# Threshold attention followed by a squared-ReLU layer on one Trainium2 core: scores a step ahead in five banks, queries loaded by sweep, values grouped by block

## The chip, the cores and the metric

The kernel runs on one core of a Trainium2 chip. A core has five engines that run their own instruction streams and meet only through semaphores: TensorE (PE in the profile, with its weight loads shown as PEld), VectorE (DVE), ScalarE (ACT), GpSimd (POOL) and SyncE (SP), whose queue here does little but issue DMAs. TensorE writes its products to PSUM, a memory of 128 partitions and 8 banks of 512 float32 each; SBUF holds everything else on the chip.

The metric is device time in microseconds (us) of one execution, as the median of several runs. A profile is one execution taken by the hardware profiler; its span runs from the first to the last recorded instruction.

## What is computed

Attention over 8 batches and 8 heads, 576 tokens, head dimension 64, in float32, whose weights are cut off below the row maximum less tau, and then a layer on the joined heads:

```python
scores = scale * np.matmul(q, k.transpose(0, 1, 3, 2))
thresh = np.max(scores, axis=-1, keepdims=True) - tau
scores = np.where(scores >= thresh, scores, -1000000000.0)
scores = scores - np.max(scores, axis=-1, keepdims=True)
attn = np.exp(scores)
attn = attn / (np.sum(attn, axis=-1, keepdims=True) + 1e-09)
attn_out = np.matmul(attn, v)
...
x = np.ascontiguousarray(attn_out.transpose(0, 2, 1, 3)).reshape(B * S, H * D)
h = x @ w_in
r = np.maximum(h, 0.0)
g = r * r
return g @ w_out
```

w_in is 512 x 2048, w_out 2048 x 512. There are 4608 tokens.

## The kernel before

**Visits and steps.** Heads are handled in pairs, two heads of 64 dimensions filling the 128 partitions. The 576 queries of a pair are five blocks: four of 128 (i = 0 to 3) and one of 64 (i = 4, where both heads share the partitions). A visit `n` is a pair with a list of blocks, and a step `s` is one block of one visit. The first batch is swept twice: visits 0 to 3 take blocks 0 and 1 (steps 0 to 7), visits 4 to 7 take blocks 2, 3 and 4 (steps 8 to 19). So the first 256 tokens of x are complete for all heads early, and the layer's work on them (chunk 0) can begin. Visits 8 to 10 take all five blocks (steps 20 to 34). In visits 0 to 10 the attention weights are turned by TensorE; from visit 11 on they are turned by DVE and DMAs ("by DMA"), and from visit 12 two visits are paired (`late_step`). The change touches visits 0 to 10.

**What a step does.** In order of the data: `scores` (L258; matmuls of L273, or L266 for block 4) puts 128 x 576 scores of each of the two heads u into PSUM; `maxima` (L310, DVE) takes the row maxima; `exponents` (ACT) makes the bias and the threshold (L322, L323) and the exponents of each head (L325); `threshold` (L337 to L340, DVE) sets the weights under the threshold to zero, by reading the scores in PSUM again, and sums them; `divide` (L345, L347, POOL) divides. Two steps later `turn` (L378) turns the weights: nine 128 x 128 transposes of TensorE in three parts of three (L386), each part copied from its PSUM bank to `wT` by ACT (L387). A step after that `mix` (L499) multiplies values with turned weights (L502) and `put` copies the sums to `xT` (L485). `prep(n)` transposes the queries and keys of a visit on DVE (L247), after `load_qk(n)` has loaded them (L179, L182); `load_v` (L230) loads values; `split_left` (L242) lays out the queries of block 4.

**Order.** It is written out by hand: an engine executes its instructions in the order in which the program issues them, and the framework puts in the semaphore waits that the data and the reuse of buffers need. The loop at L1096 writes one step after the other. In it a step issues its own scores, then the first two parts of the turn of two steps before with their copies, then its exponents, values, the third part, and threshold and division.

**PSUM.** `big` is all eight banks. Before step 10 (`early()`, L865) the scores of a step lie in banks 0 to 3 (two banks for each head, `pairs`); step 1 uses 4 to 7. Turns and values take banks 4 and 5 in alternation (`take("tx", ...)`), the second part of a turn 6 or 7. The table `AT` (L113) has four areas of 576 columns, one after the other from column 128: they span banks 0 to 4 and cross their borders. Before, only the late steps use it.

**Rounding.** The layer's weights arrive in 32 pieces, and each is brought to float32 on the way (`round_weights`, L138): stage 0 is two ACT instructions (L149, L150), stages 1 and 2 one of DVE each (L152, L154), stage 3 and the end one of POOL each (L156, L158). `end_rounding` then asks for the piece three further on. The list `pieces` says how many a step rounds: in steps 2, 4 and 6 one, from step 8 on one or two.

**The layer's work** is cut in pieces that `fill` puts between the steps' instructions at the pace of `rate` (L885). Chunk j becomes available in the step in which the last value group it needs is made (`chunk_at`); the first is step 10. `min(chunk_at)` is that step.

The lines of the timetable of value groups, in which x is a block and 3 the lag in steps:

```python
mixed = {x: (x, 3) for x in range(NBLK + 1)}
...
mixes[s + lag] = (n, cols)
```

Of the kernel before, what the change touches and what calls it, by code (L numbers as in the profile page):

```python
# [19 lines left out]
def kernel(  # L20
# [140 lines left out]
    def rows_of(n):  # L161
        return rows_in[n % 2 if n <= 2 * HP else 0]
# [3 lines left out]
    def rows_32(t, n, m):  # L166

        b, h = divmod(visits[n][0], HP)
        return t[b, 2 * h + m // 2, :, (m % 2) * 32:(m % 2) * 32 + 32].rearrange("(c p) d -> p c d", p=32)

    def load_qk(n):


        for x, t in ((rows_of(n)[1], k), (rows_of(n)[0], q)):
            for m in range(4):
                src, to = rows_32(t, n, m), x[m * 32:(m + 1) * 32, :, :]
                queue = nc.scalar if n == 0 and m % 2 else nc.sync
                last = REST // 32 if t is k and m >= 2 and not by_dma(n) else 0
                queue.dma_start(out=to[:, last:, :], in_=src[:, 0:S // 32 - last, :])  # L179
                if last:  # L180
                    queue = nc.gpsimd if n == 0 else nc.sync
                    queue.dma_start(out=to[:, 0:last, :], in_=src[:, S // 32 - last:, :])  # L182
# [61 lines left out]
    def prep_part(t, n):  # L244
        to, rows = (qT, rows_of(n)[0]) if t is q else (kT[n % 2], rows_of(n)[1])
        arrived(rows)
        nc.vector.transpose(to, rows.rearrange("p c d -> p (c d)"))  # L247

    def prep_left():
        arrived(q_left)  # L250
# [7 lines left out]
    def scores(s):  # L258


        vis, i = steps[s]
        n = 2 if i < NBLK else 1
        sc = [(second if s == 1 else pairs)[u] for u in range(n)]
        if i == NBLK:
            for half in range(2):
                nc.tensor.matmul(sc[0][:, half, 0:HALF], qmid, kT[vis % 2][:, half * HALF:(half + 1) * HALF], start=True, stop=True)  # L266
        else:
            halves = [(half, u) for half in range(2) for u in range(n)]
            if early():
                halves.sort(key=lambda x: x[1])  # L270
            for half, u in halves:
                rows = slice(u * D, (u + 1) * D)
                nc.tensor.matmul(sc[u][:, half, 0:HALF], qT[rows, i * P:(i + 1) * P],  # L273
                                 kT[vis % 2][rows, half * HALF:(half + 1) * HALF], start=True, stop=True)
        maxima(s, [x[:, :, 0:HALF] for x in sc])
# [96 lines left out]
    def keep_bank(what):  # L372
# [2 lines left out]
        kept[what] = used["bank"]  # L375
        return to

    def turn(vis, i, part):  # L378

        w = weights[vis, i][0]  # L380
        ps = take("mm", (6, 7)) if early() and part == 1 else take("tx", (4, 5))
        ps = ps.rearrange("p (c n) -> p c n", n=P)
        if i < NBLK:
            for n in range(3):
                c = 3 * part + n
                nc.tensor.transpose(ps[:, n, :], w.rearrange("p u k -> p (u k)")[:, c * P:(c + 1) * P], ident)  # L386
            nc.scalar.copy(wT[:, 2 * i:2 * i + 2, 3 * part:3 * part + 3, :].rearrange("p g c q -> p c g q"),  # L387
                           ps[:, 0:3, :].rearrange("p c (g q) -> p c g q", g=2))
        elif part < 2:
            rows = slice(part * D, (part + 1) * D)  # L390
            for c in range(NBLK):
                at = part * REST + c * P
                nc.tensor.transpose(ps[:, c, 0:D], w[rows, 0, at:at + P], ident[rows, rows])
            at = part * (NBLK + 1)
            nc.scalar.copy(wT[:, 2 * NBLK, at:at + NBLK, :], ps[:, :, 0:D])
        else:

            for rows, keys in ((slice(0, D), slice(S - REST, S)), (slice(D, P), slice(0, REST))):
                nc.tensor.matmul(ps[rows, 0, 0:D], w[rows, 0, keys], ident[rows, rows], start=True, stop=True)
            nc.scalar.copy(wT[:, 2 * NBLK, NBLK, :], ps[:, 0, 0:D])  # L400

    blocks = {}
    outside = {}
# [95 lines left out]
    def mix(n, cols):  # L499

        def term(ps, u, c, at, rows=slice(0, P), first=False, last=False):
            nc.tensor.matmul(ps[u * D:(u + 1) * D, :], vs[n % 2][rows, u * (NBLK + 1) + c, :],  # L502
                             wT[rows, at // REST:(at + ps.shape[1]) // REST, NBLK if c == NBLK else u * (NBLK + 1) + c, :],
                             start=first, stop=last)

        above, below = slice(0, D), slice(D, P)
        arrived(vs[n % 2])
        if not by_dma(n):
            ps = take("tx", (4, 5))[:, 0:cols.stop - cols.start]
            for c in range(NBLK + 1):  # L510
                for u in range(2):
                    term(ps, u, c, cols.start, first=(c == 0), last=(c == NBLK))
            put(n, cols.start, ps, False)
            return
        n1, n2 = 2 * P + REST, 2 * P
        at = ODD if paired(n) and n % 2 else ONE
        one, two = bank[0], bank[4]
        groups = (one[:, 0:n1], at, (above, below)), (two[:, 0:n2], TWO, (below, above))
        for ps, x, _ in groups:
            for c in range(NBLK):  # L520
                for u in range(2):
                    term(ps, u, c, x, first=(c == 0))

        for ps, x, places in groups:
            for u, rows in enumerate(places):
                term(ps, u, NBLK, x, rows, last=True)
        put(n, 0, one[:, ONE - at:ONE - at + 2 * P], True)
        left = ODD if at == ODD else LEFT - at
        put(n, NBLK * P, one[:, left:left + REST], False)
        put(n, 2 * P, two[:, 0:n2], True)  # L530
# [295 lines left out]
    def by_dma(n):  # L826

        return n >= 3 * HP - 1
# [7 lines left out]
    for s, (n, i) in enumerate(steps):  # L836

        if by_dma(n):
            mixed = {visits[n][1][-1]: (0, 3 if n % 2 else 4)}
        else:  # L840
            mixed = {x: (x, 3) for x in range(NBLK + 1)}
        if i in mixed:
            first, lag = mixed[i]
            cols = slice(first * P, S if by_dma(n) else min((i + 1) * P, S))
            mixes[s + lag] = (n, cols)
            g_ = visits[n][0]
            if g_ % HP == HP - 1:
                complete[s + lag] = g_ // HP * S + cols.stop
# [6 lines left out]
            j += 1  # L855
    PIECE_US = 1.76
    VALUES_US = 4.8
    SCORES_US = 1.25
    RESERVE = 3 * PIECE_US
    waiting = deque()  # L860
# [24 lines left out]
    def rate(s):  # L885


        if s < out_from:
            return PIECE_US * sum(x[2] == 0 for x in waiting) / (out_from - s)
        have = PIECE_US * len(waiting) - state["left"]  # L890
        best = 1e9
        at = s
        for e in sorted(chunk_at) + [END]:
            if e > s:
                have += sum(other(x) for x in range(at, e))
                at = e
                best = min(best, (have - (RESERVE if e < END else 0)) / (e - s))
                have += PIECE_US * sum(len(pieces_of(x)) for x in chunk_at.get(e, ()))
        return max(best, 0.0) - other(s)

    def other(s):

# [32 lines left out]
    pieces, left = [], n_pieces  # L935
    for s, (n, i) in enumerate(steps):
        if s < HP * FIRST:
            x = int(n > 0 and i == 0)
        else:
            x = 2 if (n, i) in ((2 * HP - 2, FIRST + 1), (2 * HP - 1, FIRST + 1), (2 * HP, FIRST)) else 1  # L940
        pieces.append(min(x, left))
        left -= pieces[-1]
# [59 lines left out]
    for i in range(RAW):  # L1002
        load_weights(i)
    prep(0)
    nc.vector.tensor_scalar(out=ntau8, in0=ntau8, scalar1=-1.0 / SCALE, scalar2=None, op0=ALU.mult)
    keep_busy(20)
    done = 0
    rounded_by = [0]
# [15 lines left out]
    def late_step(s):  # L1024
# [67 lines left out]
        if valued:  # L1092
            at_least(2, made)
            state["left"] = max(state["left"], -PIECE_US / 2)

    for s in range(END + 1):  # L1096
        state["step"] = s
        if s >= first_late:
            assert 4 not in kept.values()
            late_step(s)  # L1100
            continue
# [4 lines left out]
        if on:  # L1106
# [10 lines left out]
                load_qk(n + 1)  # L1117
            if now:
                round_weights(now[0], 0)
            if s != 1:  # L1120
                scores(s)
                after()
                some_later("gpsimd")
        old = steps[s - 2] if 2 <= s < NST + 2 and not by_dma(steps[s - 2][0]) else None
        at_once = now or old or early()
        lay = on and last and more and not by_dma(n) and s != 1
        if old:
            turn(*old, 0)
            turn(*old, 1)
        if on:  # L1130
            exponents(n, i)
            if s and by_dma(steps[s - 1][0]):
# [18 lines left out]
            for j in chunk_at.get(s, ()):  # L1151
                add_chunk(j)
        if old:
            turn(*old, 2)
        state["free"] = s > first_dma
        if s == 0:
            scores(1)
            prep(1)
        smooth = s > first_dma + 2 and s not in mixes
        some_later("vector")  # L1160
        some_later("gpsimd")
# [77 lines left out]
```

## Time and profile before

| what | value |
|---|---|
| runs | 1335.18, 1333.57, 1335.2 us (median 1335.18) |
| the profiled execution's own time | 1333.83 us |
| its span | 1332.0 us |
| mean granted TensorE clock | 0.994 |
| start of the scores of steps 2, 3, 4, 5 | 14.70, 21.55, 28.81, 33.60 us |
| of steps 6, 7, 8, 9 | 38.80, 43.99, 49.19, 54.39 us |
| of steps 10 and 11 | 59.73, 64.23 us |

The last three rows are the starts of the matmuls of L273 and L266 in the timeline. In the page "busy" is the time in which an engine executes; a busy TensorE is not one at its peak. A digit of the forty slices is the busy share of a fortieth of the span in tenths, and in the row of the clock the share of full speed that was granted. The chain follows the work back from the last instruction, at each step to what released it. In the timeline the columns are start, duration, engine, line, operation, output and input, count, and in brackets the idle time of the engine before it with what ended it.

### The profile page before, as it was taken

What the parts mean: (1) busy time and instruction counts of PE and PEld (TensorE: products, weight loads), DVE (VectorE), ACT (ScalarE), POOL (GpSimd) and SP (SyncE); (2) the same over time, 40 slices, a digit from 0 to 9 for tenths busy, and PEclk for the clock granted to TensorE, in tenths of its full rate; (3) what the DMA queues carried; (4) which work ended last, traced back from release to release, by engine and by line L of the source; (5) the groups of instructions that cost most, each with busy time, mean ns of one, the idle gap of its engine ahead of it and who ended that gap; (6) DMA issues with size and microseconds to landing.
All of it is one profiled execution on the core that took longest, in us unless ns stands there. A gap on an engine that the chain in (4) does not pass through costs nothing.

```text
span 1332.0 us, 25215 instructions
## 1 busy us (share of the span) xinstructions
PE 1295.4 (97%) x9112; PEld 1078.0 (81%) x9112; DVE 927.9 (70%) x2026; ACT 583.0 (44%) x1357; POOL 786.0 (59%) x915
## 2 busy tenths in 40 slices
PE   7898899999999999999999999999999999999998
PEld 5676556888787979797878878888897988889997
DVE  6877776877777878787777776868687877632131
ACT  4776674235262625343534343434443443421321
POOL 4689875775755565474665665747474747454351
PEclk7999999999999999999999999999999999999999
DMA  8764531648786968776766776676686767520000
GB/s 159 160 153 117 144 91 36 159 111 184 166 196 140 214 152 199 167 172 161 167 155 157 163 179 166 168 149 172 148 186 143 178 150 161 161 70 6 12 17 16
DMA packets 330126, 186.69 MB, mean 140 GB/s; under 512 B 291441, under 2 KB 291473, under 8 KB 323601
## 3 DMA queue, kind: packets, MB, share of 16 engines
q1 hardware_dynamic: 317696, 116.87, 46.5%
q0 software_dynamic: 10000, 67.92, 12.8%
q8 instruction: 72, 1.18, 0.4%
q10 hardware_dynamic: 2304, 0.29, 0.2%
q14 instruction: 54, 0.43, 0.1%
HBM read 109.22 MB, written 68.42 MB: 133 GB/s over the span
## 4 chain that ended last, share of the span: by engine, by line
PE 86%; DVE 4%; ACT 3%; POOL 2%; DMA 2%; issue 1%; SPq 0%; ACTq 0%; DVEq 0%; POOLq 0%
PE big L659 29%; PE big L765 28%; PE big L502 10%; PE big L289 8%; PE big L548 3%; PE big L273 3%; PE big L730 2%; PE big L386 2%; DVE st L310 1%; ACT wT L387 1%; DMA wT<-aside 1%; DVE w L337 1%; ACT w L325 1%; DMA aside<-turned 1%; POOL w L347 1%
## 5 line engine op out<-in xcount | busy, mean ns | idle before, releaser
L337 DVE SCALAR_TENSOR_TENSOR w<-big,st,w 128x576 f32<-128x576 f32 x269 | 207.1, 805 | 96.8 <-ACT w L325 96.5
L310 DVE TENSOR_REDUCE st<-big 128x1 f32<-128x576 f32 x288 | 204.2, 748 | 93.8 <-PE big L289 61.7
L347 POOL TENSOR_SCALAR w<-w,st 128x576 f32<-128x576 f32 x269 | 246.6, 926 | 26.4 <-DVE st L340 21.4
L765 PE MATMUL big<-wo,gsum 128*128 128x256 f32 x1088 | 243.8, 382 | 0.0
L765 PEld LDWEIGHTS big<-wo,gsum 128*128 128x128 f32 x1088 | 204.4, 190 | 37.0 <-issue 8.1
L659 PE MATMUL big<-xT,w_in_sb 128*128 128x128 f32 x1536 | 187.4, 277 | 1.3 <-DVE g L671 1.2
L659 PEld LDWEIGHTS big<-xT,w_in_sb 128*128 128x128 f32 x1536 | 178.5, 192 | 10.6 <-issue 8.1
L765 PE MATMUL big<-wo,g 128*128 128x256 f32 x816 | 185.3, 382 | 0.1
L325 ACT ACTIVATE w<-big,st 128x576 f32<-128x576 f32 x269 | 183.8, 734 | 0.0
L765 PEld LDWEIGHTS big<-wo,g 128*128 128x128 f32 x816 | 151.6, 190 | 26.1 <-issue 6.5
L502 PE MATMUL big<-wT,vs 128*64 128x128 f32 (+5 forms) x1700 | 164.2, 355 | 8.3 <-ACT wT L387 4.2
L502 PEld LDWEIGHTS big<-wT,vs 128*64 128x64 f32 (+1 forms) x1700 | 97.1, 137 | 72.0 <-issue 20.7
L322 ACT ACTIVATE st<-st 128x2 f32<-128x2 f32 (+1 forms) x148 | 30.3, 205 | 258.2 <-DVE st L310 257.1
L345 POOL TENSOR_SCALAR st<-st 128x2 f32<-128x2 f32 (+1 forms) x148 | 35.2, 238 | 169.3 <-DVE w L337 163.5
L408 POOL DMA_DIRECT2D aside<-turned x50 | 29.9, 597 | 177.9 <-DVE turned L437 173.7
L671 DVE TENSOR_TENSOR g<-big,g 128x512 f32<-128x512 f32 x96 | 64.7, 676 | 82.4 <-PE big L659 76.8
L289 PE MATMUL big<-kT,qT 64*128 64x256 f32 (+3 forms) x768 | 106.9, 416 | 0.0
L289 PEld LDWEIGHTS big<-kT,qT 64*128 64x128 f32 x768 | 84.5, 186 | 14.5 <-issue 5.0
L667 ACT ACTIVATE g<-g 128x512 f32<-128x512 f32 x96 | 60.2, 628 | 62.9 <-DVE g L671 62.7
L538 POOL TENSOR_TENSOR gsum<-g 128x512 f32<-128x512 f32 x34 | 46.2, 1358 | 69.8 <-ACT g L668 69.6
L668 ACT ACTIVATE g<-g 128x512 f32<-128x512 f32 x128 | 80.7, 630 | 4.1
L431 DVE STREAM_TRANSPOSE turned<-w 128x512 f32<-128x512 f32 x100 | 70.2, 702 | 0.0
(114 smaller groups left out, 2039.0 us busy)
## 6 DMA issues: line engine op xcount, KB each, us to landing
aside<-turned POOLq DMA_DIRECT2D x50, 1152.0 KB, 4.8
wT<-aside SPq DMA_DIRECT2D x200, 288.0 KB, 5.4
vs<-in_v_dram SPq DMA_DIRECT2D x72, 128.0 KB, 6.1
ql<-in_q_dram SPq DMA_DIRECT2D x126, 72.0 KB, 5.0
wo<-in_moe_w_in_dram SPq DMA_DIRECT2D x16, 512.0 KB, 4.6
wo<-in_moe_w_out_dram SPq DMA_DIRECT2D x16, 512.0 KB, 3.8
out_dram<-osb POOLq DMA_DIRECT2D x32, 256.0 KB, 3.6
kl<-in_k_dram SPq DMA_DIRECT2D x113, 72.0 KB, 2.9
```

The lines of the kernel that those rows point to most:

```text
L289: nc.tensor.matmul(big[to, at + x0:at + x1], lhsT, keys[u * D:(u + 1) * D, x0:x1], start=True, stop=True)
L310: nc.vector.tensor_reduce(out=mx[:, u:u + 1], in_=sc[u], axis=AX.XY, op=ALU.max)
L325: nc.scalar.activation(out=w[:, u, :].rearrange("p (h k) -> p h k", h=2), in_=sc[u], func=AF.Exp, bias=bias[:, u:u + 1], scale=SCALE)
L337: nc.vector.scalar_tensor_tensor(out=wu, in0=sc[u], scalar=thr[:, u:u + 1], in1=wu, op0=ALU.is_ge, op1=ALU.mult, accum_out=sm[:, u:u + 1])
L347: nc.gpsimd.tensor_scalar(out=w[:, u, :], in0=w[:, u, :], scalar1=z[:, u:u + 1], scalar2=rcp[:, u:u + 1], op0=ALU.add, op1=ALU.mult)
L431: move(wb[:, 0:h, :, :], whole_[:, 0, :, :, :])
L502: nc.tensor.matmul(ps[u * D:(u + 1) * D, :], vs[n % 2][rows, u * (NBLK + 1) + c, :], wT[rows, at // REST:(at + ps.shape[1]) // REST, NBLK ...
L659: nc.tensor.matmul(to[:, f, :], factor(j, p, q, c)[:, f * P:(f + 1) * P], part[:, c, :], start=(p in "125" and f == 0 and c == 0), stop=(p ...
L667: nc.scalar.activation(out=to, in_=to if src is None else src, func=AF.Relu)
L668: nc.scalar.activation(out=to, in_=to, func=AF.Square)
L671: nc.vector.tensor_tensor(out=x, in0=to, in1=x, op=ALU.add)
L765: nc.tensor.matmul(to, left[:, f, :], wo[:, slot, f, :], start=(f == 0), stop=(f == HF - 1))
```

## The change

Before step 10 the loop's body is replaced by `early_step`. It issues the scores of the step after, in the areas of `AT` (five banks; the areas alternate between even and odd steps), and the exponents of the step after; turns and values take banks 5, 6 and 7. ACT's order becomes: exponents of the step after, then the three copies of the turn, then stage 0 of the rounding, then the copy of the values. DVE's order is: maxima of the step after, transposes for the next visit (now in a visit's first step), threshold of the step, rounding. The early pieces are rounded in steps 3, 5 and 7 in place of 2, 4 and 6.

`load_qk` and `prep_part` handle only the queries of the sweep: 8 of 18 blocks of 32 in visits 0 to 3, 10 of 18 in visits 4 to 7. The first visit's keys are transposed in two halves, and ntau8 is scaled on POOL.

Values are made in groups: blocks 0 and 1 together in visits 0 to 3 (256 columns), 2, 3 and 4 in visits 4 to 7 (320 columns), and in visits 8 to 10 0 and 1, 2 and 3, and 4 alone. Each group is made three steps after its last block. `place_of` lays the turned weights of two neighbouring visits side by side in the sweeps. Chunk 1 becomes available in step 22 instead of 21. `rate` spreads the groups' estimated time over the steps while the rounding goes on.

```diff
+    def columns(t, n):
+        first = FIRST * P // 32
+        return slice(0, S // 32) if t is k or n >= 2 * HP else slice(0, first) if n < HP else slice(first, S // 32)
...
-                queue.dma_start(out=to[:, last:, :], in_=src[:, 0:S // 32 - last, :])
+                queue.dma_start(out=to[:, cols.start + last:cols.stop, :], in_=src[:, cols.start:cols.stop - last, :])
...
-        nc.vector.transpose(to, rows.rearrange("p c d -> p (c d)"))
+        for x in (slice(0, HALF // 32), slice(HALF // 32, S // 32)) if t is k and n == 0 else (columns(t, n),):
+            nc.vector.transpose(to[:, x.start * 32:x.stop * 32], rows[:, x, :].rearrange("p c d -> p (c d)"))
...
+        if 1 < s < min(chunk_at):
+            for u in range(n):
+                at, cut = sorted(AT.values())[2 * u + s % 2]
+                rows = slice(u * D, (u + 1) * D)
+                for x0, x1 in ((0, cut), (cut, S)):
+                    nc.tensor.matmul(big[:, at + x0:at + x1], qT[rows, i * P:(i + 1) * P], kT[vis % 2][rows, x0:x1],
+                                     start=True, stop=True)
+                sc[u] = big[:, at:at + S].rearrange("p (h k) -> p h k", h=2)
...
+    def place_of(n, i):
+        return n % 2 * 4 + 2 * i if n < HP else n % 2 * 5 + 2 * (i - FIRST) if n < 2 * HP else 2 * i
...
-        ps = take("mm", (6, 7)) if early() and part == 1 else take("tx", (4, 5))
+        to = place_of(vis, i)
+        ps = take("tx", (5, 6, 7) if early() else (4, 5))
...
-            nc.scalar.copy(wT[:, 2 * i:2 * i + 2, 3 * part:3 * part + 3, :].rearrange("p g c q -> p c g q"),
-                           ps[:, 0:3, :].rearrange("p c (g q) -> p c g q", g=2))
+            return lambda: nc.scalar.copy(wT[:, to:to + 2, 3 * part:3 * part + 3, :].rearrange("p g c q -> p c g q"),
+                                          ps[:, 0:3, :].rearrange("p c (g q) -> p c g q", g=2))
...
-            ps = take("tx", (4, 5))[:, 0:cols.stop - cols.start]
+            ps = take("tx", (5, 6, 7) if early() else (4, 5))[:, 0:cols.stop - cols.start]
+            at = place_of(n, cols.start // P) * REST
...
-            mixed = {x: (x, 3) for x in range(NBLK + 1)}
+            mixed = {1: (0, 3)} if n < HP else {NBLK: (FIRST, 3)} if n < 2 * HP else {1: (0, 3), 3: (2, 3), NBLK: (NBLK, 3)}
...
-            return PIECE_US * sum(x[2] == 0 for x in waiting) / (out_from - s)
+            return (PIECE_US * sum(x[2] == 0 for x in waiting) + sum(early_values(x) for x in range(s, out_from))) / (out_from - s) - early_values(s)
...
+    def early_values(s):
+        return EARLY_VALUES_US * (mixes[s][1].stop - mixes[s][1].start) / P if s in mixes else 0.0
...
-            x = int(n > 0 and i == 0)
+            x = int(n > 0 and i == 1)
...
-    nc.vector.tensor_scalar(out=ntau8, in0=ntau8, scalar1=-1.0 / SCALE, scalar2=None, op0=ALU.mult)
+    nc.gpsimd.tensor_scalar(out=ntau8, in0=ntau8, scalar1=-1.0 / SCALE, scalar2=None, op0=ALU.mult)
...
+    def early_step(s):
+        n, i = steps[s]
+        first = i == visits[n][1][0]
+        now = list(range(sum(pieces[:s]), sum(pieces[:s + 1])))
+        if first and n + 2 < 2 * HP:
+            load_qk(n + 2)
+        if s == 0:
+            scores(0)
+            exponents(*steps[0])
+        if s + 1 < min(chunk_at):
+            scores(s + 1)
+        if first and n < HP:
+            prep(n + 1)
+        if not first:
+            split_left(n)
+        copies = [turn(*steps[s - 2], part) for part in range(3)] if s > 1 else []
+        if s + 1 < min(chunk_at):
+            exponents(*steps[s + 1])
+        for fn in copies:
+            fn()
+        for p in now:
+            round_weights(p, 0)
+        if s in mixes:
+            mix(*mixes[s])
+        threshold(n, i)
+        for p in now:
+            for stage in (1, 2, 3):
+                round_weights(p, stage)
+        divide(n, i)
+        for p in now:
+            end_rounding(p)
+        if first and n:
+            load_v(n)
...
     for s in range(END + 1):
         state["step"] = s
+        if early():
+            rounded_by.append(state["rounded"])
+            done += pieces[s]
+            early_step(s)
+            continue
```

More of the change, by code (lines that the diff above doesn't have):

```diff
@@ L169, in rows_32 @@
         return t[b, 2 * h + m // 2, :, (m % 2) * 32:(m % 2) * 32 + 32].rearrange("(c p) d -> p c d", p=32)
+    def columns(t, n):
+        first = FIRST * P // 32
+        return slice(0, S // 32) if t is k or n >= 2 * HP else slice(0, first) if n < HP else slice(first, S // 32)
     def load_qk(n):
         for x, t in ((rows_of(n)[1], k), (rows_of(n)[0], q)):
+            cols = columns(t, n)
             for m in range(4):
@@ L263, in scores @@
         sc = [(second if s == 1 else pairs)[u] for u in range(n)]
-        if i == NBLK:
+        if 1 < s < min(chunk_at):
[6 more added lines that the diff above has]
+                sc[u] = big[:, at:at + S].rearrange("p (h k) -> p h k", h=2)
+        elif i == NBLK:
             for half in range(2):
@@ L268, in scores @@
             halves = [(half, u) for half in range(2) for u in range(n)]
-            if early():
+            if s < 2:
                 halves.sort(key=lambda x: x[1])
@@ L394, in turn @@
             at = part * (NBLK + 1)
-            nc.scalar.copy(wT[:, 2 * NBLK, at:at + NBLK, :], ps[:, :, 0:D])
+            return lambda: nc.scalar.copy(wT[:, to, at:at + NBLK, :], ps[:, :, 0:D])
         else:
@@ L399, in turn @@
                 nc.tensor.matmul(ps[rows, 0, 0:D], w[rows, 0, keys], ident[rows, rows], start=True, stop=True)
-            nc.scalar.copy(wT[:, 2 * NBLK, NBLK, :], ps[:, 0, 0:D])
+            return lambda: nc.scalar.copy(wT[:, to, NBLK, :], ps[:, 0, 0:D])
     blocks = {}
@@ L508, in mix @@
         if not by_dma(n):
-            ps = take("tx", (4, 5))[:, 0:cols.stop - cols.start]
+            ps = take("tx", (5, 6, 7) if early() else (4, 5))[:, 0:cols.stop - cols.start]
+            at = place_of(n, cols.start // P) * REST
             for c in range(NBLK + 1):
                 for u in range(2):
-                    term(ps, u, c, cols.start, first=(c == 0), last=(c == NBLK))
+                    term(ps, u, c, at, first=(c == 0), last=(c == NBLK))
             put(n, cols.start, ps, False)
@@ L857 @@
     VALUES_US = 4.8
+    EARLY_VALUES_US = 1.1
     SCORES_US = 1.25
@@ L1119 @@
                 round_weights(now[0], 0)
[L1120 to L1123, printed above, removed]
+            scores(s)
+            after()
+            some_later("gpsimd")
         old = steps[s - 2] if 2 <= s < NST + 2 and not by_dma(steps[s - 2][0]) else None
-        at_once = now or old or early()
-        lay = on and last and more and not by_dma(n) and s != 1
+        at_once = now or old
+        lay = on and last and more and not by_dma(n)
         if old:
-            turn(*old, 0)
-            turn(*old, 1)
+            turn(*old, 0)()
+            turn(*old, 1)()
         if on:
@@ L1153 @@
         if old:
-            turn(*old, 2)
+            turn(*old, 2)()
         state["free"] = s > first_dma
-        if s == 0:
-            scores(1)
-            prep(1)
         smooth = s > first_dma + 2 and s not in mixes
```

## The prediction

> **What bounds the kernel now.** I read the page first: engine sums, the forty slices, the chain's shares.
>
> ```profile
> span 1332.0 us, 25215 instructions
> PE 1295.4 (97%) x9112; PEld 1078.0 (81%) x9112; DVE 927.9 (70%) x2026; ACT 583.0 (44%) x1357; POOL 786.0 (59%) x915
> PEclk7999999999999999999999999999999999999999
> PE 86%; DVE 4%; ACT 3%; POOL 2%; DMA 2%; issue 1%; SPq 0%; ACTq 0%; DVEq 0%; POOLq 0%
> ```
>
> TensorE (PE) carries 86% of the chain, so time lost or won early moves the end one for one: what follows is PE work. The one low clock digit lies in the first slice, inside the stretch that the change rewrites. So I asked for busy times by stretch, cut where the clock changes and at the tenth step (59.7):
>
> ```profile
> 11.00:14.70 3.70, 0.00 (x0) 0.00 (x0) 3.70 (x8) 3.19 (x8) 0.00 (x0) 1.00 0.73 169
> 14.70:28.50 13.80, 12.09 (x52) 8.93 (x53) 11.01 (x27) 6.71 (x16) 8.04 (x11) 0.51 0.83 179
> 28.50:59.70 31.20, 26.89 (x225) 19.77 (x224) 25.02 (x60) 22.84 (x58) 17.83 (x24) 1.00 0.78 160
> 62.00:90.00 28.00, 27.08 (x224) 21.11 (x226) 20.63 (x47) 21.34 (x53) 23.45 (x27) 1.00 0.65 148
> 90.00:141.00 51.00, 45.09 (x378) 33.62 (x375) 38.81 (x79) 37.72 (x95) 44.09 (x45) 1.00 0.48 135
> 141.00:218.00 77.00, 73.00 (x537) 45.14 (x535) 57.37 (x133) 51.24 (x129) 57.13 (x63) 1.00 0.38 93
> ```
>
> The columns are PE, weight loads, DVE, ACT, POOL, clock, DMA share, GB/s. PE stood still for 3.7 us, and the next 13.8 us ran at half clock. No engine is full from 28.5 to 59.7; PE is near full from 62 and from 141, but not from 90 to 141. One early step in the timeline:
>
> ```profile
> 38.80 1.97 PE L273 MATMUL big<-kT,qT 64*128 64x288 f32 x8 [0.70 <-DVE w L337]
> 40.07 1.49 DVE L310 TENSOR_REDUCE st<-big 128x1 f32<-128x576 f32 x2 [0.20 <-PE big L273]
> 40.70 0.88 PE L386 MATMUL big<-ident,wo 128*128 128x128 f32 x6
> 41.28 0.86 ACT L387 COPY wT<-big 128x384 f32<-128x384 f32 x2 [1.10 <-PE big L386]
> 41.50 1.31 PE L502 MATMUL big<-wT,vs 128*64 128x128 f32 x20
> 42.34 1.37 ACT L325 ACTIVATE w<-big,st 128x576 f32<-128x576 f32 x2
> 43.11 0.82 DVE L337 SCALAR_TENSOR_TENSOR w<-big,st,w 128x576 f32<-128x576 f32 x1 [1.12 <-ACT w L325]
> 43.99 1.97 PE L273 MATMUL big<-kT,qT 64*128 64x288 f32 x8 [0.70 <-DVE w L337]
> ```
>
> A loop of 5.19 us: scores, maxima, exponents, threshold, next scores. The turn (L386) and the values (L502) run beside it, the rounding's L149 and L150 in ACT's gap (38.92 to 40.2).
>
> **What the Trainium skill says.** "TensorE: Matmul & The Clock Gate", Part 1: an idle window of about 3.4 us halves the clock, a busy one restores it. The fall agrees (3.82 us idle, then 0.50); the return took 13.4 us, past busy stretches, so I don't count on a quick one. "PSUM — Partial Sum Buffer", PSUM bank collisions: two engines may not touch the same bank and partitions at once, reads included. Before, this stage keeps each score block in its own banks; no run here shows a collision. "Perfetto Trace Analysis", Tensor Engine Instruction: ACT and DVE are strict FIFO. The trace agrees: at 94.30 L152 waited 1.13 us for L149, and the threshold stood behind it.
>
> **The change, part by part.** S(s) is the scores of step s.
>
> *Head.* The first queries are 8 of 18 blocks, the keys are transposed in halves, and ntau leaves DVE. S(0) stood at 8.57; keep_busy ends at 7.76, so it can win at most 0.8; I take 7.85. The maxima then end at about 11.87, the second visit's transposes (0.36 + 0.73) at 12.95, the threshold starts, and S(2) follows 0.88 later: 13.83 for 14.70. PE's gap is then 10.2 to 13.83, 3.6 us for 3.8.
>
> *Query loads.* Halved over both sweeps, keys unchanged; transposes fall from 0.77 to about 0.36 and 0.43. These are not in the loop: 0.
>
> *Scores ahead.* The built program's waits decide. Five banks hold four blocks of 576, so neighbours share banks: S(s+1) waits for exponents of s, and the threshold of s waits for exponents of s+1 (head by head at even s, both heads at odd). The lead is taken back. Durations: scores to end of maxima 2.75 (1.27 + 1.49), bias and thr 0.33, two exponents 1.36, threshold to next scores 0.88. S(6) to S(7) is 2.75 + 0.33 + 1.36 + 0.05 + 0.88 = 5.4, no better than 5.19.
>
> *Rounding and groups sit behind the exponents.* ACT now runs exponents, three copies, then L149 and L150; on DVE L152 and L154 wait for L149 with the next maxima behind them. In an odd step, from the end of the maxima: 1.69 to exponents' end, copies 1.25, L149 0.6, L152 and L154 0.9: 4.45. Then maxima 1.45. In an even step exponents 1.69, one copy 0.5, because the group takes the bank of the step's first turn (3 turns on 3 banks), then the group, and the next S stands behind it on PE. 256 columns: the groups of 320 and 256 in later visits took 4.72 together, 8.2 ns a column, so 2.1; I take 2.2. Then 2.75. Pair: 4.45 + 1.45 + 1.69 + 0.5 + 2.2 + 2.75 = 13.05 for 10.38, +2.7.
>
> *Walk at full clock.* S(2) at 13.83 puts the end of max(2) at 16.6 and its first exponent at 17.6: S(3) 17.65, ending at 19.45 in pieces as banks come free. Max(3) ends at 20.55, transposes of visit 2 at 21.65, and the threshold of 2 waits for the first exponent of 3, 21.65: S(4) 22.6. Max(4) ends at 25.35, its exponents wait for the turn (25.7) and end at 27.0, the threshold of 3 follows: S(5) 27.9. L154 holds max(5) to 29.8 to 31.25, exponents end at 32.95, the group runs 33.5 to 35.7: S(6) 35.75 (before 38.80, but there without a lead). Max(6) ends 38.5, and one pair later max(8) 51.55. Then 4.45 + 1.45 to max(9) 57.45, exponents 59.15, group at 59.65, turn at 61.85, S(10) 63.3 (before 59.73). Rounding of steps 8 and 9 ends at 65.85, where max(10) starts (before 61.01); step 10's own L149 and L150, turn and a 256 group (0.9 longer) follow: S(11) at 69.9 for 64.23, **+5.7**. The turn and POOL's divide don't lead there.
>
> *Clock.* If it falls in the first gap again, S lasts 3.2 for 1.6, nine turns 2.18 for 1.44, a group 4.4 for 2.2. Walked again: S(6) at 41.5 if it comes back near 31, 45.5 if only with the first group: +5.75 to +9.75. I take **+7.5**. If it holds, 0. Later gaps are about 2.5 us.
>
> *Groups later.* A group of 128 columns takes 1.28, of 64 0.77. Second-sweep visits: 2 x 1.28 + 0.77 - 2.7 = 0.63, four of them; the three full visits 2 x (2.56 - 2.2) = 0.72 each: 4.7. From 90 to 141 POOL leads the chain, two visits give nothing: **-3.4** (0 to -4.7). If the group's wait grew there it would eat this.
>
> *Nothing:* chunk 1 a step later and the fill's new rate: until the rounding ends only chunk 0 is paced. Weights are asked for a step later but land about when L149 needs them (at most +0.7). SP's value loads now precede a weight load, with a visit's time in hand.
>
> **Sum.** 5.7 + 7.5 - 3.4 = +9.8 on the profiled run's 1333.83 (span 1332.0 and 1.83 around it) = 1343.6. The median of the runs is 1.35 above: **1345**.
>
> **Rivals.**
> A, above, 0.50. For: 3.6 us idle is near the 3.82 that did it.
> B, the clock holds, 0.28: 5.7 - 3.4 = +2.3, 1337.5. For: the gap is shorter, and the window free-running by the page; against: the runs before lie within 1.7 us, so the fall looks steady.
> C, the clock stays down to step 10, 0.10: +9.75, two more groups at 2.2 each and scores at 1.6, less 3.4 with 5.7: about +18, 1353. Against: dense groups brought it back at 28.4.
> D, faster, 0.12: the groups run in PE's idle time ahead of the exponents. Then S(s+2) starts 0.94 after the first exponent, not 3.4: 2.46 saved twice and 2.2 for the third, 7.1; with the clock held 2.3 - 7.1 = -4.8, 1330.4. It decides if a group starts 2.2 us or more before the threshold ends. For: PE idles there. Against: the bank rotation.
>
> **Numbers.** Beyond 0.2% (2.7 us), about what a measurement of this kernel can tell: slower 0.68 (A, C, part of B), same 0.19 (most of B), faster 0.13 (D and tails). 1333 to 1351 leaves out D and most of C.
>
> **What would show it.** Right: L337 of a step starting when L325 of the next has ended; first groups starting 0.5 after exponents; L152 idle for L149 with L310 behind it; S(10) near 63 to 71; clock 0.50 after about 14.5. Wrong: score starts under 4.6 us apart throughout, groups beside the exponents, or S(11) before 64.2.

## The result, and the profile after

The changed kernel takes 1347.86 us (median; 1347.12 to 1348.34) beside 1334.46 us for the kernel before (1333.57 to 1335.2): 1.0100 of it, with a 95% interval of 1.0087 to 1.0113. The profiled execution took 1348.34 us, 14.5 more than that of before. The forecast was 1345, with a range of 1333 to 1351.

The page after, its engine sums, the TensorE clock by slices and the chain's shares:

```profile
span 1346.5 us, 24486 instructions
PE 1301.3 (97%) x8752; PEld 1070.4 (79%) x8752; DVE 931.5 (69%) x2026; ACT 581.4 (43%) x1339; POOL 787.3 (58%) x916
PEclk7789999999999999999999999999999999999999
PE 85%; DVE 6%; ACT 3%; DMA 3%; issue 1%; POOL 1%; SPq 0%; DVEq 0%; POOLq 0%; ACTq 0%
```

TensorE executes 360 instructions fewer than before and is busy 5.9 us longer. The clock is low in three slices of 33.7 us where it was low in one, and DVE and DMA have taken shares of the chain from PE and POOL. The clock points at the head of the run, where the windows show this (PE, weight loads, DVE, ACT, POOL, clock, DMA share, GB/s; (x247) counts instructions):

```profile
8.00:81.00 73.00, 52.33 (x247) 33.78 (x247) 46.05 (x107) 36.86 (x88) 31.36 (x41) 0.72 0.53 120
108.00:159.00 51.00, 45.46 (x273) 31.51 (x274) 40.30 (x83) 37.32 (x88) 45.37 (x47) 1.00 0.47 133
```

The mean clock is 0.72 over the whole way to step 11, which starts at 80.59 us for 64.23. So 16.4 us are lost before it, and from there to the end 1.9 are won back. The second row is the stretch in which POOL led the chain before: TensorE is as free there as it was (45.46 us busy of 51 for 45.09).

A pair of early steps in the timeline after (start, duration, engine, line, operation; in brackets the idle time before, and who ended it):

```profile
40.67 1.25 PE L276 MATMUL big<-kT,qT 64*128 64x384 f32 x8
41.85 1.20 PE L406 MATMUL big<-ident,w 128*128 128x128 f32 x9
43.70 1.35 ACT L340 ACTIVATE w<-big,st 128x576 f32<-128x576 f32 x2
45.09 0.82 DVE L352 SCALAR_TENSOR_TENSOR w<-big,st,w 128x576 f32<-128x576 f32 x1 [1.72 <-ACT w L340]
45.96 2.89 PE L276 MATMUL big<-kT,qT 64*128 64x320 f32 x8 [2.91 <-DVE w L352]
48.78 2.18 PE L406 MATMUL big<-ident,wo 128*128 128x128 f32 x9
50.21 1.59 ACT L340 ACTIVATE wo<-big,st 128x576 f32<-128x576 f32 x2
51.70 1.23 ACT L407 COPY wT<-big 128x384 f32<-128x384 f32 x3
52.23 4.53 PE L522 MATMUL big<-wT,vs 128*64 128x256 f32 x20 [1.26 <-ACT wT L407]
56.69 1.43 PE L276 MATMUL big<-kT,qT 64*128 64x384 f32 x8
```

Two things are to be seen. The order is the predicted one: the threshold (45.09) waits for the exponents of the step after it (43.70 to 45.05), the group (52.23) waits for a copy that stands behind exponents, and the scores (56.69) stand behind the group. And like work lasts twice as long on one side of 46.9 as on the other: the turn takes 1.20 and then 2.18, the group 4.53 (2.38 where the clock is full). The clock fell between, and TensorE had not stopped for longer than 2.91 us.

The early stage cut in windows of 3.41 us, laid so that a change of clock falls on an edge. (That the windows have this length comes out of the trace: the clock falls at 12.74, 29.81, 46.88, 63.95 and 77.60 us, and the distances, 17.07 and 13.65 us, are five and four times 3.413.)

```profile
9.33:12.74 3.41, 1.47 (x12) 0.96 (x8) 2.98 (x5) 1.53 (x4) 0.00 (x0) 1.00 0.55 127
12.74:16.15 3.41, 1.86 (x7) 1.54 (x8) 2.55 (x8) 1.66 (x5) 0.79 (x2) 0.50 0.96 329
...
22.98:26.39 3.41, 2.10 (x13) 1.54 (x12) 2.98 (x9) 2.87 (x7) 0.29 (x2) 1.00 0.47 83
26.39:29.80 3.41, 1.72 (x12) 1.04 (x10) 1.69 (x3) 1.99 (x6) 1.57 (x2) 1.00 0.28 64
29.80:33.22 3.42, 2.85 (x8) 1.68 (x8) 2.86 (x9) 1.91 (x5) 0.84 (x1) 0.50 0.15 34
...
43.46:46.87 3.41, 0.91 (x5) 0.74 (x6) 1.72 (x5) 3.41 (x9) 0.00 (x0) 1.00 0.02 5
46.87:50.28 3.41, 3.41 (x13) 2.33 (x12) 2.97 (x7) 0.89 (x4) 2.14 (x3) 0.50 0.49 132
...
60.52:63.94 3.42, 1.76 (x8) 1.19 (x8) 2.54 (x8) 3.00 (x7) 0.00 (x0) 1.00 0.00 0
63.94:67.35 3.41, 2.40 (x10) 1.78 (x9) 2.33 (x6) 1.93 (x5) 2.98 (x4) 0.50 0.74 193
```

In these lines a window at full clock with 1.76 us of TensorE's work or less (the first number after the length) is followed by half clock, and one with 2.10 is not. The experiments will show that busy time alone doesn't decide this. There are five stretches of half clock, 41 us together; before there was one, of 13.65 us.

### The profile page after: what moved, and what is told of

Same layout as the page of the kernel before. It is cut to its first block, busy times and chain, and to the rows that moved or that the text cites. A ratio compares the mean times of both kernels' runs of the same rounds, so it can differ in the third digit from the quotient of the medians.

```text
span 1346.5 us, 24486 instructions
## 1 busy us (share of the span) xinstructions
PE 1301.3 (97%) x8752; PEld 1070.4 (79%) x8752; DVE 931.5 (69%) x2026; ACT 581.4 (43%) x1339; POOL 787.3 (58%) x916
## 4 chain that ended last, share of the span: by engine, by line
PE 85%; DVE 6%; ACT 3%; DMA 3%; issue 1%; POOL 1%; SPq 0%; DVEq 0%; POOLq 0%; ACTq 0%
PE big L680 28%; PE big L786 27%; PE big L522 11%; PE big L304 8%; PE big L569 3%; PE big L288 2%; DVE st L325 2%; PE big L751 2%; DMA wT<-aside 1%; PE big L406 1%; DMA aside<-turned 1%; ACT w L340 1%; DVE w L352 1%; PE big L276 1%; ACT wT L407 1%
## 5 line engine op out<-in xcount | busy, mean ns | idle before, releaser
L522 PE MATMUL big<-wT,vs 128*64 128x256 f32 (+4 forms) x1340 | 164.6, 413 | 10.8 <-ACT wT L407 7.9
L522 PEld LDWEIGHTS big<-wT,vs 128*64 128x64 f32 (+1 forms) x1340 | 85.7, 140 | 80.8 <-issue 22.5
L304 PEld LDWEIGHTS big<-kT,qT 64*128 64x128 f32 x768 | 84.5, 186 | 14.5 <-issue 5.0
```

What stands on the lines that cost most here:

```text
L304: nc.tensor.matmul(big[to, at + x0:at + x1], lhsT, keys[u * D:(u + 1) * D, x0:x1], start=True, stop=True)
```

## The experiments

The order of the early steps, the clock, the value groups and the query loads were taken apart. T is the theory that the order costs some us of its own, the clock more, and that the groups give a little back. Its rivals are R1, in which the waits of the new order cost all of it and the low clock only runs beside them, and R2, in which the groups and the query loads cost it. "Filling" means transposes of the identity that nothing reads.

**1. TensorE's gaps filled** (`e1_clock`, then `e6_clock_full` with more of the same).

```diff
+    def fill_pe(times, at):
+        for x in range(times):
+            nc.tensor.transpose(big[:, at:at + P], ident, ident)
...
         copies = [turn(*steps[s - 2], part) for part in range(3)] if s > 1 else []
+        if s:
+            fill_pe(12 if s % 2 else 8, 2432 if s % 2 else 0)
```

> The changed kernel with TensorE's gaps of the early steps filled by transposes of the identity into PSUM columns that nothing reads (7 behind the scores of step 1, 8 ahead of the scores of step 2, then 12 in each odd and 8 in each even step behind the turn); nothing else moves. Theory T (the order of the early steps costs 4 to 6 us at full clock, the clock that falls in every gap some 10 more, the groups give 2 back later): the clock stays at 1.00 from about 10 us on, the scores of step 11 start at 68 to 72 us instead of 80.59, the time is 1336 to 1341. Rival R1 (the waits of the new order cost all of it, the low clock only runs beside them): 1346 to 1349, and the steps stay 10.3 us for two. Rival R2 (the value groups and the query loads cost it): 1345 or more.

Measured: 1342.47 us, ratio 1.0069 (1.0057 to 1.0082). The gain of 5.4 us is less than T expected and more than R1 allows. Step 11 starts at 76.12. The clock still fell twice. Here are a window that kept it, and one that didn't with the window after it:

```profile
42.23:45.64 3.41, 1.81 (x15) 1.57 (x14) 1.69 (x4) 2.86 (x8) 0.00 (x0) 1.00 0.15 34
...
55.88:59.29 3.41, 1.81 (x13) 1.41 (x12) 1.87 (x7) 3.41 (x8) 0.00 (x0) 1.00 0.22 48
59.29:62.71 3.42, 3.42 (x14) 2.34 (x12) 2.19 (x5) 1.04 (x4) 2.28 (x3) 0.50 0.57 146
```

Both hold 1.81 us of TensorE's work, and they end differently. Their work differs in kind: of the first window's 15 matmuls 14 are transposes, which use the whole 128 x 128 array; of the second's 13 only 7 are, and 6 are score matmuls, which use 64 of its 128 rows. The last section comes back to this.

> As e1_clock, with more transposes where it still fell to half clock (25.0 to 31.75 and 59.5 to 66.0 us): 18 in step 2, 16 in each odd and 10 in each other even step. The runs so far say that a stretch of 3.41 us with less than about 1.8 us of TensorE's work is followed by half clock. Theory T: no fall any more, the scores of step 10 start at 63 to 66 us (70.05 in e1_clock, 72.49 in the changed kernel), 1336 to 1340. R1 (the low clock only runs beside other waits): 1341 to 1344, the same as e1_clock.

Measured: 1341.96 us, 1.0059 (1.0047 to 1.0072): a miss for T by the number, and inside R1's range, so that experiments 4 and 6 have to part the two. In its profile one fall is left (14.05 to 20.88 us), and in it the filling itself became the load: 16 transposes at half clock took 3.67 us, and the scores of step 3 came at 19.85, for 17.54 in e1_clock. The steps after it ran at full clock, and steps 6 to 8 took 12.9 us for 16.0 in the changed kernel.

**2. The parts without the new order** (`e2_groups`: before with the groups of values and the change's `rate`; `e4_order_undone`: the query loads as well, with the first visit's keys in two halves and ntau8 on POOL; the name "query loads" stands for these three below).

```diff
-            mixed = {x: (x, 3) for x in range(NBLK + 1)}
+            mixed = {1: (0, 3)} if n < HP else {NBLK: (FIRST, 3)} if n < 2 * HP else {1: (0, 3), 3: (2, 3), NBLK: (NBLK, 3)}
```

> The kernel before with the groups of values alone. T: 1331.5 to 1333.5, the gain coming between steps 11 and 30. R2: 1338 or more. The difference from the run with the query loads too is what those loads give: T expects 0 to 0.5 us.

> The kernel before with the groups of values and the query loads of the change, and its own order of the early steps. T and R1: 1331.5 to 1333.5, about 2 us under the kernel before. R2: 1340 or more.

Measured: 1338.35 us (1.0033; 1.0020 to 1.0046) and 1336.20 us (1.0017; 1.0010 to 1.0023), with 1333.88 for before beside them. T was wrong on both, and R2's number was met by the first (1338 or more), not by the second (1340 or more): the groups, which leave TensorE less to do, cost 4.5 us. The windows of the second kernel suggest why, and experiment 4 tests it:

```profile
24.34:27.75 3.41, 1.37 (x10) 1.02 (x9) 2.33 (x6) 3.35 (x9) 2.00 (x3) 0.99 0.52 102
27.75:31.16 3.41, 3.41 (x12) 2.13 (x10) 2.02 (x5) 0.77 (x2) 1.75 (x3) 0.50 1.06 235
...
37.99:41.40 3.41, 1.11 (x6) 0.92 (x6) 3.24 (x9) 3.31 (x8) 1.99 (x3) 0.99 0.64 137
41.40:44.82 3.42, 3.42 (x13) 2.10 (x12) 1.85 (x3) 0.82 (x3) 1.63 (x2) 0.50 0.49 79
```

The kernel before, in the same stretch:

```profile
38.59:42.00 3.41, 3.20 (x24) 2.43 (x26) 3.13 (x9) 2.31 (x6) 2.93 (x4) 1.00 0.92 186
42.00:45.42 3.42, 2.72 (x26) 2.09 (x23) 2.24 (x8) 2.25 (x7) 0.00 (x0) 1.00 0.50 79
```

A group of 128 columns in every early step (1.31 us) kept each window here above 2.7 us of work. With one group of 256 in every second step the steps between have no group, a window there holds 1.1 to 1.4 us, and the clock falls every 13.65 us, which is four windows.

**3. The group ahead of its own turn** (`e5_group_ahead`). In this kernel the turn's third part is written over the group before ACT copies it, so the first 256 tokens get turned weights in place of values; the time is that of the same instructions.

```diff
+        into_x = mix(*mixes[s]) if s in mixes else None
         copies = [turn(*steps[s - 2], part) for part in range(3)] if s > 1 else []
...
-        if s in mixes:
-            mix(*mixes[s])
+        if into_x:
+            into_x()
```

> The changed kernel with the group of values put ahead of the step's own turn on TensorE, so that it no longer takes a bank that a copy behind the exponents frees; its copy into the tokens stays behind the exponents on ACT. T: the scores after a group start 2.5 to 5 us earlier after the group's own scores, three groups in the early steps, and gaps of TensorE stay, so the clock may still fall: 1337 to 1344. R1: 1334 to 1338, since the wait of the groups is most of the loss. R2: 1346 or more.

Measured: 1347.42 us, 1.0099 (1.0085 to 1.0113): no gain, against T and R1 and as R2 had it. Its clock falls four times, so it doesn't tell what the wait costs at full clock; experiment 6 took that up.

**4. The clock held where the groups are** (`e7_both`: e4_order_undone with filled gaps; `e8_before_clock`: before with its one gap filled; `e11_loads_held`: the latter and the query loads).

```diff
             turn(*old, 2)
+            if s in (2, 3, 5, 7, 9):
+                fill_pe(14, (7 - used['mm'] % 2) * 512 + 3 * P)
```

> The kernel e4_order_undone (the order of before, the groups and query loads of the change) with transposes of the identity, which nothing reads, in TensorE's gaps: 7 behind the scores of step 1, 8 ahead of those of step 2, 10 behind those of step 2, 14 at the end of steps 2, 3, 5, 7 and 9. T with the clock rule (five falls are all that the groups cost): clock 1.00 from 10 us on, scores of step 10 at 54 to 58 us for 67.39, 1323 to 1328. R2 (the groups cost by their own waits): 1334 or more.

> The kernel before with such transposes up to step 3 only, where its one fall of the clock lies (14.9 to 28.4 us); the groups of 128 columns in every step from 3 on are left to hold it. T: no fall, 1328 to 1331. R1: 1333 to 1335.

> The kernel before with the query loads of the change and the transposes of e8_before_clock, its own groups of 128 columns kept. T (the loads give 1.2 to 2.2 us, as between e2_groups and e4_order_undone): 1329 to 1330.5. The distance to e7_both is then what the groups give where the clock is held: 3.5 to 5 us. Rival: groups give nothing even so, and this one reaches 1326 as well.

Measured: 1325.54 us (0.9937; 0.9925 to 0.9949), 1331.32 (0.9983; 0.9977 to 0.9990; 0.3 above T's range) and 1330.41 (0.9974; 0.9963 to 0.9985). The first is the fastest kernel of the study, 22.3 us under the changed one, with the change's values and loads in the old order and 95 transposes more. Beside e4_order_undone, from which it differs by these transposes alone, it wins 10.7 us, so what the low clock costs there is shown. Its page and its early stage:

```profile
span 1323.1 us, 24664 instructions
...
PEclk9999999999999999999999999999999999999999
```

```profile
8.00:59.00 51.00, 46.06 (x320) 34.85 (x319) 42.10 (x101) 35.73 (x86) 28.56 (x36) 1.00 0.73 155
```

```profile
48.37 2.38 PE L521 MATMUL big<-wT,vs 128*64 128x256 f32 x20
...
51.16 1.68 PE L280 MATMUL big<-kT,qT 64*128 64x288 f32 x8
52.77 1.20 PE L405 MATMUL big<-ident,wo 128*128 128x128 f32 x9
53.80 1.69 PE L331 MATMUL big<-ident 128*128 128x128 f32 x14
56.21 1.24 PE L273 MATMUL big<-kT,qmid 128*128 128x288 f32 x4 [0.71 <-ACT qmid L248]
```

No digit of the clock is low, the group takes 2.38 us for the 3.97 to 4.39 of e4_order_undone, and the transposes (L331) lie in a gap that is there anyway. So at a held clock the groups, with their `rate`, are worth 1330.41 - 1325.54 = 4.9 us to the good, where without it they cost 4.5: the sign of this part is the clock's, and R2 is wrong about the groups' own waits. All of the 4.9 is won behind step 11, which starts at 61.16 us here and at 61.26 with groups of 128; the stretch to step 30 then takes 114.6 for 120.7. (The pacing that experiment 5 looks at comes along with the groups in this order.) The query loads give 0.9 here (the intervals of e8_before_clock and e11_loads_held overlap) and 2.15 between the two kernels of experiment 2.

**5. The pacing** (`e9_left`).

```diff
+        if s == min(chunk_at):
+            state["left"] = 0.91
         state["usable"] = rounded_by[-1]
```

> The changed kernel with one number set: at step 10 the pacing of the first tokens' products starts with 0.91 us in hand, which is what the early loop of before leaves there with the groups of the change, and not with 0; the instructions behind step 10 then stand in the same order as in e4_order_undone. T (behind step 10 e4_order_undone won 4.5 us on the kernel before and the changed kernel lost 1.7, and pacing is the only difference of order there): 1341.5 to 1345. If the late loss is the rounding or the loads running behind instead: 1347 or more.

Measured: 1343.67 us, 1.0071 (1.0058 to 1.0085), 4.2 us under the changed kernel, as T expected. From the scores of step 11 to those of step 30, first the changed kernel, then this one:

```profile
80.59:199.39 118.80, 110.37 (x648) 71.58 (x647) 91.35 (x192) 85.54 (x201) 99.51 (x105) 1.00 0.50 131
```

```profile
79.53:194.24 114.71, 108.64 (x648) 71.00 (x647) 92.95 (x192) 85.79 (x201) 99.00 (x105) 1.00 0.53 136
```

The same 648 matmuls, in another order among the steps, take 4.1 us less, and TensorE's idle time falls from 8.4 to 6.1 us. In the kernel before the stretch takes 120.6. The early loop of before calls `fill` in every step. With its own `rate`, which counts waiting pieces alone, nothing adds up there; with the change's `rate`, which counts the groups ahead, 0.91 us are in hand at step 10 (e2_groups, e4_order_undone). The change's own early loop calls `fill` no more and enters step 10 with 0.

**6. Clock and pacing together, and the group's wait** (`e12_held_left`; on it `e10_group_first` and `e13_group_bank`, two ways in which the group waits for no copy of its own step). In e10 the group stands ahead of the turn, as in experiment 3; in e13 it takes the rest of the bank of the turn's last part:

```diff
-            ps = take("tx", (5, 6, 7) if early() else (4, 5))[:, 0:cols.stop - cols.start]
+            ps = bank[(5, 6, 7)[used["tx"] % 3]][:, P:] if early() else take("tx", (4, 5))
+            ps = ps[:, 0:cols.stop - cols.start]
```

> The changed kernel with both things that the runs so far found to cost: TensorE's gaps filled as in e6_clock_full (12 instead of 16 transposes in step 1, where the fill itself ran into half clock there), and the 0.91 us in hand at step 10 of e9_left. T (the two add up): 1342 less 4.2, and up to 2 less for the head: 1335.5 to 1338.5, with the scores of step 10 at 64.5 to 66.5 us; what is left above e7_both, about 11 us, is the order of the early steps at full clock. If they don't add up: 1340 or more.

> e12_held_left with the group of values ahead of the step's own turn, its copy into the tokens ahead of the next exponents, and the turn's third part behind that copy, so that the group waits for no exponents of its step (4 transposes instead of 10 fill the even steps). The prediction's step that groups stand behind the exponents (about 2.2 us of each pair of steps): an even step from scores to scores falls from 7.6 to about 6.5 us, the scores of step 10 come 3 to 4.5 us earlier than in e12_held_left, and the time is 1332 to 1335. If the shared banks alone hold the steps: no more than 1 us under e12_held_left.

> e12_held_left with the early turns split 4, 4 and 1 over their three banks and the group of values written beside the one, so that it follows the turn at once and waits for no copy behind the exponents; its own copy is the last of the step (2 transposes instead of 10 fill the even steps from 4 on). In e10_group_first the group stood ahead of the turn, and the next exponents, which write into the weights that the turn reads, waited for both: that wait took the place of the old one. The prediction's step (groups behind exponents cost about 2.2 us of each pair): an even step takes 5.3 to 5.8 us for 7.6, the scores of step 10 come 5 to 7 us earlier than in e12_held_left, 1330 to 1333. If the shared banks and the rounding hold the even steps anyway: over 7 us for them, 1336 or more.

Measured: 1337.66 us (1.0026; 1.0016 to 1.0036), 1337.88 (1.0027; 1.0018 to 1.0037), 1338.54 (1.0031; 1.0020 to 1.0043). Clock and pacing add up: 10.2 us off the changed kernel, where filling alone took 5.9 (e6_clock_full) and pacing alone 4.2. Moving the group gave nothing, so both times the number is that of the rival expectation. The even steps did become shorter, 7.60 (scores of step 7 to those of step 8) to 6.84 (e10) and 6.77 us (e13), but less than expected. In both profiles the clock fell near 26 us, where e12_held_left kept it, and in e13 again at 69.88. In e13 the filling itself seems to hold the step: the two transposes behind the group end near 51.0 us, and the threshold, which shares their bank, starts at 51.09 though the exponents that it waits for ended at 50.1. (The profile names a copy of ACT that ended at 51.03, so this is not shown.) So what the group's wait costs was not separated from the rest.

One more wait shows in e12_held_left; in the changed kernel, at its lower clock, the same transposes waited for no DMA:

```profile
22.87 0.45 DVE L254 STREAM_TRANSPOSE qT<-ql 128x256 f32<-128x256 f32 x1 [2.80 <-DMA ql<-in_q_dram]
...
24.74 1.44 PE L276 MATMUL big<-kT,qT 64*128 64x384 f32 x6 [2.71 <-DVE w L359]
```

The third visit's queries land at 22.87, DVE stands 2.80 us for them, and the threshold behind the transposes releases the scores of step 4 only at 24.74.

## Why the prediction was right, and where not

The sign and the range hold: the order costs and the low clock costs about as much again. Two terms were mis-sized, and the course of the clock was another than the predicted one, so that its size came out by luck. By its steps, with e12_held_left as the changed order at nearly full clock:

- **The head.** In the changed kernel itself step 0 starts at 7.69 (predicted 7.85), step 2 at 14.28 (13.83): the first maxima ended 0.64 later, behind matmuls of 3.11 us.
- **The order, +5.7 at step 11.** Step 11 starts at 72.78 there, 8.55 later than before; the term was 2.9 too small. Its parts: scores 6 to 7 5.28 (predicted 5.4), the pair 12.88 (13.05). Step 4 was expected at 22.6 and came at 24.74, for want of the queries: the step "these are not in the loop: 0" failed here. A fall of the clock from 57.84 to 61.26 is in the rest, and so is what the filling itself holds up (the threshold at 16.73 waits 0.77 us behind transposes).
- **The clock, +7.5.** The changed kernel reaches step 11 another 7.8 us later than e12_held_left; e9_left, with the same pacing, 6.75. The size was right, the course was not, and that is luck. The prediction let the clock fall once, return by 31 us or with the first group, and dismissed the rest with "Later gaps are about 2.5 us". They were (2.1 to 2.9 us), but the clock came back at 22.98 us, earlier than either, and fell four more times, after windows with gaps of that size and too little work.
- **Groups later, -3.4.** The changed kernel won 1.85 us from step 11 to the end. The step that failed is the one put under "Nothing", "the fill's new rate": with 0.91 us in hand the steps from 11 to 30 gain 5.9 us on before, with 0 only 1.8. The 5.9 is more than the 4.7 which the groups' durations gave for all visits, so that two visits would give nothing in the stretch led by POOL is not borne out either; with the changes POOL holds 15% of the chain from 108 to 159 us, for 45% from 90 to 141 before.
- **Query loads, 0.** With the halved keys and ntau8 they are worth 0.9 to 2.15 us, at the head: in e4_order_undone step 0 starts at 7.48 for 8.57 and step 2 at 13.28 for 14.70. The prediction counted such a gain in its head; no run has the loads alone.
- **Rounding behind exponents.** L152 waited for L149 in steps 8 and 9 alone (0.47 and 2.71 us). The 4.45 us from one end of maxima to the next start in an odd step came out (40.40 to 44.77 in e12_held_left), but by another path: threshold and rounding follow each other on DVE without a wait for ACT's rounding.
- **The sum.** 8.55 + 7.8 - 1.85 = 14.5 for the predicted 9.8: the two misses, 2.9 and 1.55, went the same way, and 0.3 is the clock's.
- **The rivals.** B wanted a held clock; e12_held_left nearly holds it and lands at B's 1337.5, but by other terms: a dearer order, and a later gain that needs the pacing. C's clock that stays down to step 10 did not come, five stretches did. D's groups ahead of the exponents gave nothing in e5_group_ahead, e10_group_first or e13_group_bank, in each of which the clock fell as well.

What the forecast did not see at all is how the parts share the loss. Against the kernel before with the same groups, loads, pacing and a held clock (e7_both), the new order costs 1337.66 - 1325.54 = 12.1 us, with one fall of the clock in it. Half clock costs the kernel before 2.8 us (e8_before_clock), and the groups and loads could give 5.8 at a held clock. The change joined a fast part and a slow one, and neither of them held the clock.

The Trainium skill ("TensorE: Matmul & The Clock Gate", Part 1) speaks of an idle window of about 3.4 us. The length agrees: falls in e4_order_undone are 13.65 us apart, four times 3.41. That the window has to be idle does not: here windows that were about half busy were enough, and in one run one with 2.25 us of work, and the measurement decides.

## What to carry to other kernels

Cut TensorE's time into windows of the clock's own length and look at the work in each, not at the longest gap, and count a matmul that uses half of the array as half: merging small matmul groups into rare large ones can cost more in clock than it saves in instructions. Where a gap can't be closed, a few transposes that nothing reads hold the clock, if they end before anything that has to wait for them is due (in e12_held_left a threshold waited 0.77 us for them). And when a loop or its pacing is rewritten, follow what the pacing variables hold where the next loop begins.

## What had not been expected of the hardware

- TensorE's busy time alone does not tell whether the clock falls. At full clock, windows of 3.41 us with 1.73 (e12_held_left) and 1.81 us (e1_clock) kept it, and others with 1.81 and up to 2.25 us lost it. From e12_held_left, one of each, and the window after the second:

```profile
20.30:23.71 3.41, 1.73 (x16) 1.49 (x14) 0.84 (x2) 2.58 (x7) 0.25 (x1) 1.00 0.42 67
...
54.43:57.84 3.41, 2.25 (x12) 1.30 (x11) 2.74 (x9) 2.79 (x6) 0.00 (x0) 1.00 0.00 0
57.84:61.25 3.41, 3.41 (x18) 3.41 (x18) 1.23 (x2) 2.15 (x6) 3.17 (x5) 0.50 0.87 200
```

- The share of the array does tell. Multiply the columns that a matmul streams by the share of the 128 x 128 array that its weights fill: the scores of the 128-row blocks (64 x 128) and value groups (128 x 64) count half, whole transposes in full. The two windows above come to 1931 and 1413 such columns. Summed over every window from 7 us on in the 14 traces, with matmuls across an edge divided by time, the 45 windows at full clock that were followed by half clock hold 1484 or fewer, and the 5321 that were not hold 1536 or more. This was worked out from the finished traces, and no run was made to test it. Busy time, columns alone, or columns with only the rows or only the weights' columns counted do not separate them.
- The way back has nearly the same border. Up to 1300 us, before TensorE runs out of work, 39 windows at half clock with 1543 such columns or fewer stayed there, and 31 with 1555 or more were followed by full clock. So a window can be busy throughout and not bring the clock back: 46.87 to 50.28 in the changed kernel holds 1506. There the way back took one to three windows (3.4 to 10.2 us), in e5_group_ahead up to seven (14.46 to 38.35 us).
